# Half of gate and value by seven half products, a fixed order of instructions, and first loads in halves

## The chip, the cores and the metric

The kernel runs on one core of a Trainium2 chip. The metric is the device time of one execution in microseconds; lower is better. Three timed runs of the kernel before gave 265.98, 265.60 and 265.23 us, a median of 265.6 us. A core has a matrix engine (TensorE, PE in the profile), two engines for elementwise work (VectorE, DVE; ScalarE, ACT), a general engine (POOL) and one that mostly issues transfers (SP). Each takes its own instructions in order; they wait for one another by semaphores. Matmuls write into PSUM, eight banks of 512 float32 per partition, and both elementwise engines read from there.

## The reference

```python
# causal attention: q, k, v are [4 batches, 8 heads, 768 tokens, 64]
scores = matmul(q, k.transpose(0, 1, 3, 2)) / 8
# heads 0, 2, 6: every key up to the query
# the other five: the last 64 keys and the first 4 ("sinks")
a = softmax(where(mask, scores, -1e9))
x = matmul(a, v)                       # -> [3072 tokens, 512]
# feed-forward, weights 512 x 1536, 512 x 1536, 1536 x 512, 512 x 512
g   = x @ w_gate
val = x @ w_val
ffn = (gelu(g) * val) @ w_out
out = x + sigmoid(x @ w_res) * ffn
```

## The kernel before

**Tiling.** The 3072 tokens are six chunks of 512 (CHUNKS), numbered 0 to 5. A chunk's attention is computed for pairs of heads, then its feed-forward, while the attention of the next chunk is mixed in between. Everything that TensorE multiplies is float16, sums are float32.

**Stages of a chunk.** Queries and keys are brought into transposed form, by TensorE for the first chunks (`loads_rows`, L672; qks staging tiles, qkt results) and by transposing transfers of SP for the later ones (`loads_natural`, L732, dT). Scores go to PSUM (L893, sink scores L984), ACT takes the exponential (L909), VectorE masks. TensorE weighs the values (L1017 for the windows of streaming heads). The windows of 64 keys need the values shifted by 64 rows, which a copy `vs` makes from the value tile `va` (by ACT or VectorE for the first chunk, by SP's transfers later, L662). The keys and queries of head pair 1 are wanted on the lower partitions too; the transfer `q6` (L762) moves them. VectorE normalises; x stays in `xtok` as float32, and TensorE transposes a float16 copy to `xT` (L1106), 4 blocks of 128 features by 512 tokens.

**Gate and value.** `gate_value` (L1121) handles the 1536 features in twelve blocks of 128 (f = 0 to 11). For each block gate and value are 4 matmuls of 128x128 by 512 tokens each (one for each of 4 blocks of x's features), through the helper `mm` (L514 to L517). In the later chunks `mm` splits a matmul into two of 64 columns, so as to keep the tile shape of the attention's matmuls next to it; that is L517, the full one is L516. ACT takes gelu from the gate's bank to `gact` (L1166), VectorE multiplies it with the value's bank and 0.5 into `hT` (L1168).

**Output.** Two token tiles of chunk 0 use the plain product (`output`). All others use `output_fast` (L1212): for two tiles of 128 tokens, [h] · w_out is cut into halves three ways (tokens, the inner 1536 features in even and odd blocks, 256 columns) and made of seven half products instead of eight (the form of Strassen and Winograd). With A the tokens' halves and B the weights', it needs sums of h (`sums`, L1175: S1 to S4, four VectorE instructions per part, L1187), sums of w_out (`weight_sums`, L1199: T1 to T4 in `wt`, four planes), copies of partial results from PSUM to an output tile `otile` (keep, L1251 and L1252) and additions to it (plus, L1257). Then come x @ w_res with tanh (srs, L1226), the gated product (L1281), the addition of x (L1286) and a transfer of 256 KB to `out` (L1292) by SP: 128 tokens x 512 columns each.

**Loads.** POOL issues all loads from HBM (`dma`, L577): these cast float32 to float16. SP issues what moves inside the core and the outputs. The first loads are, in POOL's order: queries and keys of chunk 0 for heads 0 to 3, then for heads 4 to 7 (4 loads of 512 KB), its four value tiles, the first third of w_gate and of w_val, and so on; w_res and w_out follow.

**What sets the order.** The program is a list of tasks with dependencies. `schedule` (L219) plays them through with modelled durations and picks for each free engine the ready task with the lowest priority value; for TensorE a task that keeps the tile shape goes first. `HINTS` (L49) overwrites some priorities by task number. Tasks made with `flex` (copies out of PSUM, some additions) go to the engine that would be done sooner. Buffers come out of pools (SBUF tiles, PSUM banks by kind) at the moment when a task is scheduled. A loop at the end adds orders between a chunk's phases (gate-value after scores, the next chunk's scores after block 10). `warm` matmuls (L1333) fill the time until the first gate product.

Of the kernel before, what the change touches and what calls it, by code (L numbers as in the profile page):

```python
# [4 lines left out]
NHEAD = 8  # L5
SEQ = 768
# [37 lines left out]


HINTS = (
    "3:-58.9 11:-130.04 428:854.14 430:718.61 444:2782.08 457:-821.9 460:407.45 490:4205.68 521:1522.06 "
    "591:-818.43 610:-36.63 612:486.89 613:-2965.25 619:1544.03 621:-44.07 643:467.87 644:-881 646:4.3 656:119.6 "
    "664:25.04 673:629.62 675:-109.25 695:-2674.26 696:-1856.67 703:-881.5 706:-108.75 707:714.39 708:1939.7 "  # L49
    "711:270.02 712:497.18 716:476.22 720:652.56 738:638.32 743:520.23 744:3053.24 749:514.3 750:1799.28 "  # L50
    "751:2383.53 756:521.28 762:1469.72 764:4344.87 767:2237.74 787:-603.93 815:5053.25 817:2978.67 821:1231.87 "
    "824:1484.86 836:2402.62 837:798.1 841:706.04 848:-288.52 849:2997.07 876:2751.74 906:2555.54 913:1516.93 "
    "918:2437.99 919:1519.88 924:1537.25 931:1510.23 936:2384.32 949:2443.79 955:2089.28 967:2846.74 995:-227.38 "
    "1001:29.83 1002:3171.86 1003:3180.29 1004:1146.58 1007:2686.58 1012:1781.89 1040:-803.29 1043:1907.45 "
    "1045:1028.83 1046:667.33 1050:3229.28 1051:1536.45 1053:3573.03 1056:-1823.77 1084:4090.27 1110:2454.97 "
    "1111:2597.62 1117:2808.38 1123:2507.5 1128:2481.58 1129:2529.63 1134:2508.5 1146:2434.73 1152:2779.33 "
    "1153:3034.61 1158:3861.94 1165:2795.06 1171:3076.63 1176:2997.8 1185:5989.69 1188:2243.92 1189:2528.84 "
    "1192:2789.39 1193:2537.45 1194:3836.22 1208:3021.15 1215:6294.68 1263:3219.13 1268:5037.38 1283:4420.5 "
    "1308:4756.92 1311:3513.6 1317:3517.03 1321:3052.3 1329:5930.49 1330:3507.5 1335:3508.5 1336:3519.22 "
    "1341:4624.14 1345:3444.6 1353:3516.64 1354:3538.83 1357:2761.66 1365:3787.63 1366:5173.04 1372:5102.72 "  # L60
    "1386:5438.32 1392:4014.31 1393:4933.66 1418:5146.68 1430:4133.91 1441:5428.8 1452:5127.54 1457:2188.42 "
    "1462:4595.33 1464:5711.23 1467:9389.54 1468:4425.54 ~1471:550.69 1476:5611.77 1499:4504.13 1513:6742.83 "
    "1516:5340.27 1522:4510.5 1523:4585.63 1526:3632.38 1534:4503.02 1539:4253.34 1550:4463.64 1565:7711.51 "
    "1570:4506.5 1571:5085.34 1580:2427.42 1594:2466.44 1610:9272.71 1625:3048.93 1627:6036.71 1629:6167.81 "
    "1631:5064.12 1644:6476.5 1662:4125.72 1671:5044.95 1672:7314.6 1676:4967.2 1683:6427.71 1692:9540.12 "
    "1711:7387.16 1757:5137.62 1784:5507.1 1797:5469.41 1803:7562.23 1817:7773.49 1818:7478.69 1823:7672.83 "
    "1834:7419.08 1836:10250.4 1849:7490.55 "
)

# [31 lines left out]
class Buf:  # L101
    __slots__ = ("pool", "kind", "slot", "left", "users", "war", "free_at")

    def __init__(self, pool, kind=None):
        self.pool, self.kind = pool, kind
        self.slot = None
        self.left = 0
        self.users = []
        self.war = []
        self.free_at = 0.0  # L110


class Pool:
# [14 lines left out]

    def take(self, buf, t):
        best = min(x for x in self.free if x[0] <= t)  # L130
# [13 lines left out]
class Psum:  # L144
# [23 lines left out]

    def take(self, buf, t):
# [18 lines left out]
SWITCH = 0.1  # L188
SWAP = -3000.0
VK_AT = -18.5  # L190
VS_DMA = 0
LAT = {"pe": 0.20, "act": 0.10, "dve": 0.08, "pool": 0.12, "sp": 0.1}


# [1250 lines left out]
```

The softmax here doesn't subtract the row's maximum and nothing guards it: scores larger than these inputs give would overflow.

## Time and profile before

| | |
|---|---|
| timed runs | 265.98, 265.60, 265.23 us |
| profiled execution: span from first to last instruction | 263.7 us |
| around the span (median of the runs less the span) | 1.9 us |
| TensorE busy | 257.7 us, 3226 matmuls |
| VectorE, ACT, POOL busy | 181.6, 147.2, 89.3 us |
| gelu on ACT (L1166), 512 wide | 68 x 597 ns |
| product on VectorE (L1168), 512 wide | 68 x 686 ns |
| transfers | 29.22 MB, 111 GB/s in the mean |

The profile comes from one execution, whose own time beside its span isn't listed; the 1.9 us are a difference between it and other executions. A busy share is a mean over the span; which engine sets the end is read from the chain of work that ended last. An engine's busy time is made of instructions that may overlap: TensorE's matmuls are pipelined, so the distance between two starts is the price of one, and not its length. Times of groups are given as a sum and a mean of one; the shapes behind a group tell which rows may be compared.

### The profile page before, as it was taken

What the parts mean: (1) busy time and instruction counts of PE and PEld (TensorE: products, weight loads), DVE (VectorE), ACT (ScalarE), POOL (GpSimd) and SP (SyncE); (2) the same over time, 40 slices, a digit from 0 to 9 for tenths busy, and PEclk for the clock granted to TensorE, in tenths of its full rate; (3) what the DMA queues carried; (4) which work ended last, traced back from release to release, by engine and by line L of the source; (5) the groups of instructions that cost most, each with busy time, mean ns of one, the idle gap of its engine ahead of it and who ended that gap; (6) DMA issues with size and microseconds to landing.
All of it is one profiled execution on the core that took longest, in us unless ns stands there. A gap on an engine that the chain in (4) does not pass through costs nothing.

```text
span 263.7 us, 7495 instructions
## 1 busy us (share of the span) xinstructions
PE 257.7 (98%) x3226; PEld 164.0 (62%) x3226; DVE 181.6 (69%) x378; ACT 147.2 (56%) x237; POOL 89.3 (34%) x127
## 2 busy tenths in 40 slices
PE   7999999999999999999999999999999999999993
PEld 6777655468444668544567444589655588655692
DVE  2698437798447888557898366888557689837655
ACT  2785467974244987423787242967243888233430
POOL 8999979506109973975000000000000000000003
PEclk9999999999999999999999999999999999999999
DMA  6999999999999999999996110004200004200003
GB/s 83 174 204 206 188 175 231 175 153 204 134 200 148 165 137 177 171 179 176 174 156 150 42 40 0 2 26 101 82 2 0 2 2 122 82 2 0 2 35 127
DMA packets 96513, 29.22 MB, mean 111 GB/s; under 512 B 84449, under 2 KB 93025, under 8 KB 96481
## 3 DMA queue, kind: packets, MB, share of 16 engines
q0 software_dynamic: 70320, 14.69, 67.5%
q1 hardware_dynamic: 26160, 14.07, 28.0%
q8 instruction: 25, 0.41, 0.7%
q14 instruction: 8, 0.06, 0.1%
HBM read 29.36 MB, written 6.29 MB: 135 GB/s over the span
## 4 chain that ended last, share of the span: by engine, by line
PE 95%; DMA 2%; DVE 1%; issue 0%; POOLq 0%
PE ps L516 50%; PE ps L517 32%; PE ps L893 5%; PE ps L1333 2%; PE ps L1017 2%; PE ps L709 2%; DMA qks<-in_q_dram 2%; PE ps L1106 2%; PE ps L984 1%; DVE otile L1281 1%; DVE otile L1286 1%; DVE otile L1257 0%; POOLq L1427 0%
## 5 line engine op out<-in xcount | busy, mean ns | idle before, releaser
L1166 ACT ACTIVATE gact<-ps 128x512 f16<-128x512 f32 x68 | 40.2, 597 | 73.5 <-PE ps L516 43.7
L1168 DVE SCALAR_TENSOR_TENSOR hT<-gact,ps 128x512 f16<-128x512 f16 x68 | 46.1, 686 | 48.0 <-PE ps L516 23.1
L516 PE MATMUL ps<-xT,wg 128*128 128x512 f16 (+1 forms) x208 | 50.0, 363 | 0.0
L516 PE MATMUL ps<-xT,wv 128*128 128x512 f16 (+1 forms) x202 | 49.0, 362 | 0.0
L1286 POOL TENSOR_TENSOR otile<-otile,xtok 128x256 f32<-128x256 f32 x3 | 2.4, 801 | 136.2 <-DVE otile L1281 136.2
L577 POOL DMA_DIRECT2D qks<-in_k_dram x36 | 28.0, 810 | 17.3 <-DMA qkt<-qks 13.9
L516 PEld LDWEIGHTS ps<-xT,wg 128*128 128x128 f16 x208 | 20.1, 98 | 20.0 <-DVE otile L1257 0.3
L516 PEld LDWEIGHTS ps<-xT,wv 128*128 128x128 f16 x202 | 19.4, 98 | 20.0 <-DVE hT L1168 0.5
L577 POOL DMA_DIRECT2D qks<-in_q_dram x36 | 28.4, 828 | 2.2 <-issue 1.4
L517 PE MATMUL ps<-xT,wv 128*64 128x512 f16 x204 | 28.3, 380 | 0.0
L577 POOL DMA_DIRECT2D va<-in_v_dram x24 | 21.3, 920 | 15.1 <-PE ps L516 15.1
L517 PE MATMUL ps<-xT,wg 128*64 128x512 f16 x192 | 26.3, 379 | 0.0
L909 ACT ACTIVATE ea<-ps 128x1024 f16<-128x1024 f32 (+2 forms) x24 | 21.1, 915 | 1.7 <-PE ps L893 1.6
L1257 DVE TENSOR_TENSOR otile<-otile,ps 128x256 f32<-128x256 f32 x33 | 13.6, 417 | 7.1 <-PE ps L517 4.7
L1226 ACT ACTIVATE srs<-ps 128x512 f32<-128x512 f32 x22 | 13.1, 595 | 9.1 <-PE ps L517 6.7
L517 PEld LDWEIGHTS ps<-xT,wv 128*64 128x64 f16 x204 | 11.5, 110 | 9.8 <-DVE hT L1168 0.3
L1084 DVE TENSOR_TENSOR xtok<-ps,rcp 128x512 f32<-128x512 f32 (+1 forms) x28 | 16.8, 606 | 0.2
L517 PEld LDWEIGHTS ps<-xT,wg 128*64 128x64 f16 x192 | 11.1, 110 | 9.0
L893 PE MATMUL ps<-qkt 64*128 64x64 f16 (+4 forms) x391 | 16.4, 213 | 0.0
L893 PEld LDWEIGHTS ps<-qkt 64*128 64x128 f16 x391 | 9.8, 94 | 8.0 <-issue 4.2
L516 PE MATMUL ps<-wo,hT 128*128 128x256 f16 (+1 forms) x84 | 14.4, 304 | 0.0
L1286 DVE TENSOR_TENSOR otile<-otile,xtok 128x512 f32<-128x512 f32 (+1 forms) x21 | 14.3, 691 | 0.2
(109 smaller groups left out, 437.4 us busy)
## 6 DMA issues: line engine op xcount, KB each, us to landing
out_dram<-otile SPq DMA_DIRECT2D x22, 256.0 KB, 2.4
va<-in_v_dram POOLq DMA_DIRECT2D x24, 128.0 KB, 17.6
qks<-in_k_dram POOLq DMA_DIRECT2D x32, 64.0 KB, 12.6
qks<-in_q_dram POOLq DMA_DIRECT2D x32, 64.0 KB, 13.0
wg<-in_moe_w_gate_dram POOLq DMA_DIRECT2D x3, 512.0 KB, 10.2
wv<-in_moe_w_val_dram POOLq DMA_DIRECT2D x3, 512.0 KB, 12.1
wo<-in_moe_w_out_dram POOLq DMA_DIRECT2D x4, 384.0 KB, 22.8
vs<-va SPq DMA_DIRECT2D x4, 260.0 KB, 7.9
```

The lines of the kernel that those rows point to most:

```text
L516: return e.matmul(o, lhsT=lhsT, rhs=rhs, **k)
L517: return [e.matmul(o[h:h + 64], lhsT=lhsT[:, h:h + 64], rhs=rhs, **k) for h in (0, 64)][-1]
L577: return G.add(eng, issue, lambda e: e.dma_start(out_ap(), in_ap), deps, prio, bufs=bufs, dma=cost, name=name, grp=grp)
L709: return [e.transpose(out=at16(scr)[64 * x:64 * x + 64, (m * n + i) * 128:(m * n + i + 1) * 128], in_=piece(jj, h, i), identity=ident[:, : ...
L893: return [e.matmul(at(scr)[:, oo:oo + w], lhsT=side(BB, low, 1)[half, k0:k0 + 128], rhs=side(BB, low, 0)[half, qq:qq + w], start=True, sto ...
L909: return e.activation(out=o, in_=i_, func=AF.Exp, scale=SM_SCALE)
L1084: t2 = G.add("dve", c_dve(2 * n * 64), lambda e: e.tensor_tensor(out=xview(), in0=avv(0, DHEAD), in1=scale(), op=ALU.mult), [t1] + xdeps, ...
L1166: ta = G.add("act", c_act(512), (lambda gb=gb, ga=ga: lambda e: e.activation(out=at(ga)[:, :], in_=at(gb)[:, :], func=AF.Gelu))(), [tg], p ...
L1168: th = G.add("dve", c_dve(512), (lambda vb=vb, ga=ga, f=f: lambda e: e.scalar_tensor_tensor(out=hv(f), in0=at(ga)[:, :], scalar=0.5, in1=a ...
L1226: tas.append(G.add("act", c_act(512), (lambda rb=rb, sr=sr: lambda e: e.activation(out=at(sr)[:, :], in_=at(rb)[:, :], func=AF.Tanh, scale ...
L1257: return G.add("dve", c_dve(256), lambda e: e.tensor_tensor(out=dst(), in0=dst(), in1=at(D)[:, 0:256], op=ALU.add), [t, k], pr, bufs=[D, o ...
L1286: fn = (lambda ot=ot, lt=lt, w=w: lambda e: e.tensor_tensor(out=at(ot)[:, w], in0=at(ot)[:, w], in1=at(xbuf)[:, lt, w], op=ALU.add))()
```

## The change

1. **Seven half products for the blocks 6 to 11 of gate and value, chunks 1 to 5** (`fast`). Blocks 6, 7, 8 are paired with 9, 10, 11. For each pair, gate and value each become one group: halves of the tokens (256), of x's features (two blocks of 128) and of the output features (the two blocks). Each product is two matmuls of 128x128 by 256. Three *lanes* of two PSUM banks hold the groups in turn. Between the products a copy within PSUM (seed), a copy to an `otile` buffer (hold) and two additions (merge) do what keep and plus do in `output_fast`. The sums of x (xS, four per chunk) and of the weights (`gv_sums`, eight in all, T3 in place of the weight block) are made by VectorE. gelu and product then read both halves of a block from the two banks of the lane in one instruction.
2. **Fixed order.** `HINTS` is empty. `PLAN` lists for each engine the numbers of its tasks in order (TensorE, ACT, VectorE, POOL, SP) and for each buffer its place. `schedule` follows the lists. The loop over phases is gone; some modelled durations differ.
3. **First chunk's queries and keys** are loaded in halves of 256 tokens: six loads in POOL's order, the second half of the queries (512 KB) ahead, then keys and queries of the first half for heads 0 to 3 and 4 to 7 (256 KB each), then the keys' second half. qkt is split into a tile for keys and one of 512 wide for a chunk's queries; `q6` becomes two transfers; `vs` copies seven of eight heads.
4. **x stored early in chunks 1 to 4** (ACCUM, `store_x`). SP writes x (1 MB) to `out` as soon as it is there; the 16 output tiles of these chunks then are added to it by accumulating transfers that POOL issues, and the addition of x on VectorE falls away.
5. **Small things.** w_out's T3 replaces its block, `wt` has three planes; hS is split into two tiles, the smaller shared with xS; two srs buffers instead of three; warm matmuls are 256 wide and 70 instead of 124; the last outputs may be issued by ACT's queue (one is).

In the built programs TensorE has 3434 matmuls instead of 3226, VectorE 454 instructions instead of 378, ACT 282 instead of 225, POOL 141 instead of 123, SP 72 instead of 80.

```diff
+VS = (NHEAD - 1) * (DHEAD + 1)
+NP = 3
+FA, FB = NF - 2 * NP, NF - NP
+LANES = 3
...
+PLAN = (
...
+ACCUM = range(1, 5)
...
+        lists = [[int(x) for x in line.split()] for line in "".join(PLAN).split("/")] if PLAN else []
+        queue = {e: [self.tasks[x] for x in xs] for e, xs in zip(ENGS, lists)}
+        if queue:
+            bufs = dict.fromkeys(b for t in self.tasks for b in t.bufs)
+            assert len(bufs) == len(lists[5])
+            for b, x in zip(bufs, lists[5]):
+                b.fixed = x if x >= 0 else None
...
-                for t in cand[e]:
+                offers = cand[e]
+                if queue:
+                    offers = [t for t in queue[e][heads[e]:heads[e] + 1] if t in offers] + [t for t in offers if t.name == "warm"][:1]
...
+        "lane": (LANES, [(4, 5), (2, 3), (0, 1)]),
...
+        for y in range((z - a) // 2):
+            lo = (a + 2 * y) * 128
+            for gi, (h0, h1) in enumerate(((0, 4), (4, 8)) if c == 0 and y == 0 else ((0, 8),)):
+                for j, src in ((1, k), (0, q)):
+                    t = dma("pool", base + 4 * gi + 8 * y + 1 - j, (h1 - h0) * n * (0.092 if c else 0.089),
+                            (lambda j=j, h0=h0, h1=h1, y=y: lambda: sv(j, h0, h1, y))(),
+                            src[b, h0:h1, lo:lo + 256, :].rearrange("h (p j) d -> p h (j d)", j=n), bufs=[st[j]])
+                    t.late = 1.0 if c else 0.0
+                    for h in range(h0, h1):
+                        tok[j, h, y] = t
         values(b, a, z, base + (10 if c == 0 else 2), False, c == 0)
...
+    def gv_sums():
+        for nm, w in (("g", wg), ("v", wv)):
+            wt_ = gvt[nm]
+            blk = lambda k, j: w[:, 2 * k:2 * k + 2, (FB if j else FA) * 128:(FB if j else FA) * 128 + NP * 128]
+            here = [wtok[nm, j] for j in range(3)]
+            def add(o, x, y, deps, k):
+                return G.add("dve", c_dve(NP * 256, 2, False), lambda e: e.tensor_tensor(out=o, in0=x, in1=y, op=ALU.subtract),
+                             deps, 910 + k, name=f"{nm}T")
+            t1 = add(wt_[:, 0], blk(0, 1), blk(0, 0), here, 0)
+            t2 = add(wt_[:, 1], blk(1, 1), wt_[:, 0], [t1] + here, 1)
+            t4 = add(wt_[:, 2], blk(1, 0), wt_[:, 1], [t2] + here, 2)
+            t3 = add(blk(0, 1), blk(1, 1), blk(0, 1), [t1] + here + gv_tail, 3)
+            gvtok[nm] = {"T1": t1, "T2": t2, "T3": t3, "T4": t4}
...
+        for q in range(2 * NP):
+            j, nm = q // 2, "gv"[q % 2]
+            fa, fb, w, wt_ = FA + j, FB + j, (wg, wv)[q % 2], gvt[nm]
+            blk = lambda k2, f, w=w: lambda k: w[:, 2 * k2 + k, f * 128:(f + 1) * 128]
+            tw = lambda x, wt_=wt_, j=j: lambda k: wt_[:, x, k, j * 128:(j + 1) * 128]
+            right = {"B11": blk(0, fa), "B21": blk(1, fa), "B22": blk(1, fb), "T3": blk(0, fb), "T1": tw(0), "T2": tw(1), "T4": tw(2)}
+            lane = lanes_[q % LANES]
+            ps, free = lane
+            es = Buf(P_ot)
+            AL, AR, BL, BR = (slice(x * 256, x * 256 + 256) for x in range(4))
+            name, p_ = f"{nm}{fa}", pr + 6 + q
+            def product(parts, deps, extra=(), ps=ps, left=left, right=right, name=name, p_=p_):
+                need = [x for l, r, _, _ in parts for x in ([stok[l]] if l[0] == "S" else xd) + ([gvtok[nm][r]] if r[0] == "T" else [])]
+                t = G.add("pe", c_mm(256, 2 * len(parts)), lambda e: [
+                    mm(e, at(ps)[:, D], lhsT=right[r](k), rhs=left[l](k), start=first and k == 0, stop=(k == 1), skip_group_check=True)
+                    for l, r, D, first in parts for k in range(2)], need + deps, p_, bufs=[ps, xtbuf, xs] + list(extra), name=name)
...
+            def copy(o, i, deps, bufs, nm_):
+                return G.flex({"act": (c_act(256), lambda e: e.activation(out=o(), in_=i(), func=AF.Copy)),
+                               "dve": (c_dve(256), lambda e: e.tensor_copy(out=o(), in_=i()))}, deps, p_, bufs=bufs, name=nm_)
+            def merge(o, deps, ps=ps, es=es):
+                return G.add("dve", c_dve(256), lambda e: e.tensor_tensor(out=at(ps)[:, o], in0=at(ps)[:, BL], in1=at(es)[:, 0:256], op=ALU.add),
+                             deps, p_, bufs=[ps, es], name="merge")
+            t15 = product([("A11", "B11", AL, True), ("S1", "T1", AR, False)], list(free))
+            seed = copy((lambda ps=ps: at(ps)[:, BL]), (lambda ps=ps: at(ps)[:, AL]), [t15], [ps], "seed")
+            hold = copy((lambda es=es: at(es)[:, 0:256]), (lambda ps=ps: at(ps)[:, AR]), [seed], [ps, es], "hold")
+            t6 = product([("S2", "T2", BL, False)], [seed])
+            m1 = merge(AR, [t6, hold])
+            t7 = product([("S3", "T3", BL, False)], [m1])
+            t23 = product([("A12", "B21", AL, False), ("S4", "B22", AR, False)], [m1])
+            m2 = merge(BR, [t7])
+            t4 = product([("A22", "T4", BL, False)], [m2])
...
+                if nm == "g":
+                    ga = gas[f] = Buf(P_ga)
+                    ta = G.add("act", c_act(512), (lambda x=x, ga=ga, both=both: lambda e: e.activation(
+                        out=two(at(ga)[:, :]), in_=both(x), func=AF.Gelu))(), done + [t4], p_, bufs=[ps, ga], fset="gelu", name=f"gelu{f}")
...
+        t1 = add(wt[:, 0], w(0, 1), w(0, 0), tall, 1)
+        t2 = add(wt[:, 1], w(1, 1), wt[:, 0], [t1], 2)
+        add(w(0, 1), w(1, 1), w(0, 1), tall + [t1] + plain, 3)
+        add(wt[:, 2], w(1, 0), wt[:, 1], [t2], 4)
...
+    def store_x(c, xbuf, xtoks):
+        n = 2 if c == len(CHUNKS) - 1 else 4
+        r0 = c * 512
+        stored[c] = G.add("sp", 0.65, lambda e: e.dma_start(
+            out[r0:r0 + n * 128, :].rearrange("(i p) d -> p i d", p=128), at(xbuf)[:, 0:n, :]),
+            list(dict.fromkeys(t for i in range(n) for t in xtoks[i])), 1000 * c - 3500, bufs=[xbuf], dma=0.65 * n, name="xst")
+        stored[c].late = 1.0
...
+            if c in ACCUM and not end:
+                t = G.add("pool", 1.0, (lambda ot=ot, r0=r0: lambda e: e.dma_start(out[r0:r0 + 128, :], at(ot)[:, :], accum_op=ALU.add))(),
+                          ends + [stored[c]], pr - 3000, bufs=[ot], dma=1.0, name="out")
+                t.late = 2.0 if c < 4 else 1.5
+                continue
...
+        if c in ACCUM:
+            store_x(c, xbuf, xtoks)
```

## The prediction

> **What bounds the kernel now.** I read the page first, then the chain in order of time, TensorE's timeline, single stretches, and last the groups with their shapes.
>
> ```profile
> span 263.7 us, 7495 instructions
> ...
> PE 257.7 (98%) x3226; PEld 164.0 (62%) x3226; DVE 181.6 (69%) x378; ACT 147.2 (56%) x237; POOL 89.3 (34%) x127
> ...
> PEclk9999999999999999999999999999999999999999
> DMA  6999999999999999999996110004200004200003
> ...
> PE 95%; DMA 2%; DVE 1%; issue 0%; POOLq 0%
> ```
>
> TensorE is busy 98% and makes 95% of the chain, at full granted clock in every slice. The transfers are near their limit for the first 22 slices (145 us) and idle after. The chain in order of time (start, length, what) says where TensorE is not the bound:
>
> ```profile
> 1.32 4.32 DMA qks<-in_q_dram
> ...
> 24.92 11.25 PE ps L516 x64
> ...
> 105.16 0.03 issue
> ...
> 257.37 0.42 DVE otile L1257
> ...
> 259.33 1.01 DVE otile L1281 x3
> 260.37 0.77 DVE otile L1286
> ```
>
> Up to 24.9 us it waits for loads; from there to 259.3 us no link names another engine for more than a few hundredths; then follows a tail of 4.3 us. So between 24.9 and 259.3 us a microsecond of matmul removed is a microsecond won, unless a new wait eats it. Two prices come from TensorE's timeline (start, length, what):
>
> ```profile
> 68.69 1.03 PE L516 MATMUL ps<-xT,wg 128*128 128x512 f16 x4
> 69.55 1.03 PE L516 MATMUL ps<-xT,wv 128*128 128x512 f16 x4
> ...
> 93.67 0.82 PE L516 MATMUL ps<-wt,hT 128*128 128x256 f16 x6
> 94.42 0.61 PE L893 MATMUL ps<-qkt 64*128 64x128 f16 x10
> ```
>
> Starts count, not lengths. Four matmuls of 512 columns take 69.55 − 68.69 = 0.86 us, 216 ns each. Six of 256 take 0.75 us: 6 × 109 ns (their spacing inside the group) plus about 0.10 us, which every change of the tile's shape (here 128*128 to 64*128) costs. Pairs of 64-column matmuls (the late chunks) cost per pair the same as one full matmul. With these prices for every matmul in the written order I get 245.1 us for TensorE's stream; the trace is that stream shifted by 12.3 us at the dense start and 14.2 us at the end, so under 2 us of waits lie between.
>
> **The change part by part, against the profiled execution's 263.7 us of span.**
>
> *Seven half products.* One group covers gate (or value) of two 128-feature blocks for 512 tokens. Before: 2 × 4 matmuls of 512 = 8 × 216 = 1.728 us. After: 7 products × 2 = 14 of 256 = 14 × 109 = 1.526 us. Saved 0.202 us; three pairs, gate and value, five chunks make 30 groups: −6.06 us. The new order has 106 changes of tile shape instead of 99: +7 × 0.10 = +0.7. Together **−5.4**; the new list priced in full gives 239.9 us, −5.2.
>
> Here a rule speaks against the change. "TensorE: Matmul & The Clock Gate" of the Trainium skill, section "Back-to-back issue gap", gives for a sustained stream of weight load and matmul about 81 ns at 128 columns and 131 ns at 512, that is some 98 ns at 256 between them. By it a group goes from 8 × 131 = 1.05 to 14 × 98 = 1.37 us, 30 × 0.32 = +9.7 us, and the kernel to about 275. The rows decide: 216 and 109 ns are measured in this stream, weight loads included, so a half-width matmul costs half.
>
> *What each group asks of the others.* A copy from PSUM to PSUM (seed), one to an output tile (hold), and two additions (merge) on VectorE. Nearest rows by shape:
>
> ```profile
> L1257 DVE TENSOR_TENSOR otile<-otile,ps 128x256 f32<-128x256 f32 x33 | 13.6, 417 | 7.1 <-PE ps L517 4.7 <-PE ps L516 2.0
> L1286 DVE TENSOR_TENSOR otile<-otile,xtok 128x512 f32<-128x512 f32 x20 | 13.4, 684 | 0.2
> ...
> L1187 DVE TENSOR_TENSOR hS<-hT 128x512 f16<-128x512 f16 x6 | 2.6, 426 | 0.2
> ```
>
> A 256-wide ACT copy out of PSUM takes 0.380 us (L1252). VectorE: 60 merges × 0.417 = 25.0, 16 seeds and holds × 0.42 = 6.8, 20 sums of x × 0.42 = 8.4, eight weight sums × 0.55 (between the 0.42 of 512 and the 0.95 of 1536 elements, L1204) = 4.4; away go 16 additions of x × 0.684 = 10.9, about eight keeps that move to ACT (3.4), and some 2.9 of smaller copies: 181.6 + 27.4 = 209 us. ACT: 44 seeds and holds × 0.38 = 16.7, the keeps 3, small things 1.9: 147.2 + 21.6 = 169 us. In the stretch of chunk 3 (stretch and length; busy PE, weight loads, VectorE, ACT, POOL; granted clock, DMA share, GB/s):
>
> ```profile
> 128.14:165.25 37.11, 37.11 (x356) 21.63 (x357) 27.00 (x55) 20.91 (x32) 0.00 (x0) 1.00 0.57 88
> ```
>
> VectorE goes from 27.0 to 27.0 + 12 × 0.417 + 4 × 0.42 + 3 × 0.42 − 4 × 0.684 = 32.2 us, in a chunk that shrinks to about 36: 90%. It fits, with little room.
>
> *New waits.* TensorE takes its list in order. Product 6 waits for the seed, 7 and the 2+3 pair for the first merge, 4 for the second: 90 waits, and whatever stands behind on TensorE waits too. One link costs 0.20 us (last matmul to the engine's start, as before a gelu) + 0.38 to 0.42 + 0.05 back = 0.64 to 0.68 us. In the new order other matmuls stand between the steps: at least 0.87 us nearly everywhere, 0.65 once. That is the cover; without it 90 × 0.65 = +58 us. About 30 of the waits have 0.9 us or less, where one instruction of 0.69 us just begun on VectorE makes it late. Ends: 0, and 30 × 0.12 = +3.6 (half of 0.69 less the 0.23 of margin). The nearest row is the output stage, which already lives with copies and additions between its products, and where TensorE shows no idle time with VectorE at 73% of the chunk; so near the lower end: **+0.4**.
>
> *First loads in halves.* The order on POOL's queue becomes: six loads of queries and keys, two value tiles, w_val's first third, a query load of chunk 1, two value tiles, w_gate's first third. Before, the first two weight loads landed at 16.88 and 19.43 us, and the first gate product started at 19.72, behind 7.37 us of other matmuls. Now w_gate has 512 KB more ahead of it (1.43 us by the first loads' landing intervals): about 21 to 22 us; the first gate product has 1.9 us more matmuls ahead of it and would start at 21.6 with before's gaps. Ends −0.3 and +0.9; I take **+0.3**. That the first scores can start earlier only moves work within this wait.
>
> *Shifted values of chunk 1.* Their copy waits for value tiles which now stand behind w_out's four loads. Counting POOL's bytes at the 175 GB/s of those slices, the tiles land near 52 us; a copy on SP's queue takes 5.3 to 8 us (page: 7.9 median), so 57.3 to 59; the windows of chunk 1 want it at 57.8. Before it landed at 45.1 for a need at 56.4. Ends 0 and +2.5; **+0.6**.
>
> *x stored early, outputs accumulated.* Four stores of 1 MB on SP, which stand ahead of transposes, vs and q6 of the next chunk there; and 16 accumulating outputs on POOL, ahead of one value and two query loads of chunk 3. "DMA: Bandwidth & Descriptors" of the skill, section "Issuing engines are not separate DMA queues", says that all issuers share the same engines and interleave; the trace agrees where both queues are at work (the 9s of the DMA row). So the store of chunk 1 costs the loads about 6 us (1 MB at 175 GB/s) rather than nothing. Chunk 2's q6 had 1.24 us of slack (landed 88.56, used 89.79); now I put need at 90.5 and landing at 85 to 90: ends 0 and +3, **+0.2**. Chunk 3 had over 15 us, and after slice 22 the engines idle. The queries behind the accumulating outputs keep an estimated 7 us.
>
> *The rest at nothing.* The first chunk's weight sums run beside its output matmuls; two result buffers instead of three and the split hS stand under the same matmuls; the tail stays at 4.3 us, since the last four outputs keep their additions; fewer warm-ups only fill the wait for loads.
>
> Sum: −5.4 + 0.4 + 0.3 + 0.6 + 0.2 = −3.9. Span 263.7 − 3.9 = 259.8; the timed runs lie 1.9 us above the span (median 265.6), so **261.7 us**.
>
> **The rivals.**
> *All waits covered.* Only the stream's −5.4 counts: 260.2. For it: no idle on TensorE before. Against it: three tight places at once.
> *VectorE becomes the bound in the gate-value stage.* 30 late merges × 0.12 = +3.6 instead of 0.4: 264.9, anywhere from 263.2 to 266. For it: 90% load and 30 thin covers; against it: ACT can carry seeds, and the stage between (scores, windows) lets VectorE catch up.
> *Slower: POOL's queue stops at the first accumulating output.* It waits for the store of x and for chunk 1's last gated value; behind it stand chunk 3's queries. If the store lands late (it shares the engines with all loads), the scores of chunk 3 start late. From about 7 us late it costs time, from 11 us late it has eaten the 3.9; at 14 us late the kernel takes about 268.7. For it: 9s in the DMA row until 145 us; against it: those loads need only be in at about 127 us.
> *The folding does not do what it says* (half-width matmuls at more than half the price, as in the rule above): 275, and the 109 ns row excludes it.
>
> **How the numbers follow.** The likeliest case (260.6 to 263.2) 0.54; all covered 0.20; VectorE the bound 0.15, of which 0.05 end within 0.8 us of before; POOL's queue 0.10; anything else 0.01. 0.3% of 265.6 is 0.8 us, about what a measurement of this kernel tells from no change. Faster: 0.54 + 0.20 + 0.10 and the odd 0.01 = 0.85; same 0.05; slower 0.10. The range goes from below the covered case (all ends low: −5.4 − 0.3, 259.9, and 0.3 of spread) to 264.6, where most of the third case is in.
>
> **What would show it.** Right: matmul starts 109 ns apart in the new groups; TensorE's busy time near 252 us at 97 to 98%; VectorE near 209, ACT near 169; TensorE idle before the products with merges and seeds under 0.5 us in sum, before the first gate product at 21 to 22 us, before chunk 1's windows near 57 us. Wrong: idle before the merged products in every chunk with VectorE at 95% (third case), idle before the scores of chunk 3 released by a DMA (fourth), or a later dense start than 26 us.

## The result

The changed kernel is slower: over the runs of one chip its ratio to the kernel before is 1.0056 (95% interval 1.0033 to 1.0079), medians 268.54 and 265.84 us. The ratio leaves out its three longest executions (270.48, 272.1 and 275.8 us), which count as slow because they lie over 1.5% above its fastest; the medians are of all seven. Its executions scatter much more (266.2 to 275.8 us, before 265.2 to 266.8), and the profiled one, at 270.48 us, is among the longer; the reading below says which waits vary. In a later comparison the same kernel had 1.0201 (1.0141 to 1.0262).

The page of the profile after:

```profile
span 268.7 us, 8098 instructions
...
PE 255.6 (95%) x3434; PEld 180.5 (67%) x3434; DVE 206.6 (77%) x454; ACT 165.6 (62%) x293; POOL 106.6 (40%) x145
...
PEclk9999999999999999999999799999999999999999
DMA  7999999998989999999909999347473019340004
...
PE 70%; DMA 14%; POOL 11%; ACT 2%; issue 2%; DVE 1%; POOLq 0%; DVEq 0%
```

TensorE is no longer 95% of the chain but 70%; transfers and POOL, which issues them, hold a quarter. The transfer row has 9s up to 168 us (slices of 6.7 us; before up to 138 us), with an empty slice from 134 to 141 us, and the slice after 148 us shows a lower TensorE clock. What TensorE waited for in the whole execution, its three largest waits (engine, line, releaser: us in total, times, longest):

```profile
PE ps L616 <- DMA xT<-x: 2.2, 1, 2.2
PE ps L1137 <- issue: 2.0, 1, 2.0
PE ps L1137 <- DMA vs<-va: 1.3, 1, 1.3
...
```

Three single waits, none on a merge. The chain in order of time places them:

```profile
31.15 21.46 DMA va<-in_v_dram
...
52.62 7.84 DMA vs<-va
...
60.51 0.44 PE ps L1137 x16
...
141.83 8.45 DMA xT<-x
150.32 9.89 PE ps L616 x50
...
226.09 1.96 issue
228.04 0.35 PE ps L1137 x11
```

At 60.5 us chunk 1's windows wait for the shifted values; at 150.3 us chunk 3's gate products wait for transposed x, a transfer that took 8.45 us (3.2 us in the median before); at 226 us TensorE stops for 2 us in the middle of a group, waiting for nothing that the profile shows.

TensorE's stream, priced as in the prediction, is 239.9 us, and the trace follows it except at a few places. The *shift* is how much later a matmul starts in the trace than it would if the stream ran without a wait. The first row gives the streams, the second the shift at the dense start, each later row what is added to the time in that stretch (us; the last matmul's 0.1 us stands in the first row and in the last but one):

| stretch | before | after | difference |
|---|---|---|---|
| stream of matmuls | 245.1 | 239.9 | −5.2 |
| shift at the dense start (27 us) | 12.42 | 13.99 | +1.6 |
| 27 to 62 us (chunk 1's windows) | 0.26 | 1.50 | +1.2 |
| 62 to 140 us | 0.72 | 1.11 | +0.4 |
| 140 to 151 us (chunk 3's transposed x) | 0.04 | 2.43 | +2.4 |
| 151 to 162 us (lower clock, one merge) | 0.0 | 1.93 | +1.9 |
| 162 us to the last matmul, without the next | 0.81 | 0.70 | −0.1 |
| the stop at 226 us | 0.0 | 2.2 | +2.2 |
| from the last matmul's start to the end | 4.4 | 5.1 | +0.7 |
| span | 263.7 | 268.7 | +5.0 |

This is the account of one long execution. Without the two rows from 140 to 162 us its span would be 264.4 us and its time 266.2 us (1.8 us lie around this span: 270.48 − 268.7); the fastest execution took 266.15 us. So by this estimate the start, chunk 1's windows, the stop at 226 us and the tail already cancel the gain, and the two rows are most of the scatter. No short execution of this kernel was profiled, so this is a fit and not a measurement.

The lower clock, in TensorE's timeline after the wait at 150 us:

```profile
150.77 2.94 PE L616 MATMUL ps<-xT,wg 128*128 128x512 f16 x8
153.50 1.70 PE L616 MATMUL ps<-xT,wv 128*128 128x512 f16 x4
155.04 0.38 PE L616 MATMUL ps<-xT,wg 128*128 128x256 f16 x2
```

Eight matmuls take 2.73 us and four 1.54, where 216 ns each would make 1.73 and 0.86; so the difference is that of eight matmuls at 0.43 us. The granted clock from 151.5 to 154.8 us is 0.50. 426.7 ns at 512 columns is what the Trainium skill ("TensorE: Matmul & The Clock Gate", section "Wait — 56ns, not 53.3ns?") gives for the cold clock, so row and page agree; the price is 1.00 + 0.68 = 1.7 us on top of the wait.

### The profile page after: what moved, and what is told of

It is laid out like the page before. It is cut to its first block, busy times and chain, and to the rows that moved or that the text cites. A ratio compares the mean times of both kernels' runs of the same rounds, so it can differ in the third digit from the quotient of the medians.

```text
span 268.7 us, 8098 instructions
## 1 busy us (share of the span) xinstructions
PE 255.6 (95%) x3434; PEld 180.5 (67%) x3434; DVE 206.6 (77%) x454; ACT 165.6 (62%) x293; POOL 106.6 (40%) x145
## 4 chain that ended last, share of the span: by engine, by line
PE 70%; DMA 14%; POOL 11%; ACT 2%; issue 2%; DVE 1%; POOLq 0%; DVEq 0%
PE ps L617 32%; PE ps L616 31%; DMA va<-in_v_dram 8%; POOL qks L678 4%; PE ps L1013 3%; DMA xT<-x 3%; DMA vs<-va 3%; POOL va L678 2%; PE ps L1137 1%; POOL wo L678 1%; PE ps L1226 1%; POOL wg L678 1%; POOL wv L678 1%; POOL m_win L636 0%; ACT L1111 0%
## 5 line engine op out<-in xcount | busy, mean ns | idle before, releaser
L1523 POOL DMA_DIRECT2D out_dram<-otile x16 | 14.9, 1014 | 87.8 <-DVE otile L1519 77.6
L616 PE MATMUL ps<-xT,wg 128*128 128x512 f16 (+1 forms) x172 | 40.1, 344 | 0.0
L616 PE MATMUL ps<-xT,wv 128*128 128x512 f16 (+1 forms) x162 | 37.2, 341 | 2.2 <-DMA xT<-x 2.2
L678 POOL DMA_DIRECT2D qks<-in_k_dram x37 | 31.4, 873 | 10.4 <-DMA kT<-qks 10.4
L1366 DVE TENSOR_TENSOR ps<-ps,otile 128x256 f32<-128x256 f32 x60 | 24.7, 429 | 7.2 <-PE ps L616 3.4
L616 PEld LDWEIGHTS ps<-xT,wv 128*128 128x128 f16 x162 | 15.8, 99 | 14.4 <-DMA xT<-x 2.7
L1029 ACT ACTIVATE ea<-ps 128x1024 f16<-128x1024 f32 (+2 forms) x24 | 21.4, 920 | 3.2 <-PE ps L1013 3.2
L617 PE MATMUL ps<-xT,wv 128*64 128x512 f16 (+1 forms) x164 | 20.1, 346 | 0.0
L616 PE MATMUL ps<-wo,hT 128*128 128x256 f16 (+1 forms) x114 | 19.2, 296 | 0.2 <-ACT otile L1490 0.2
L617 PE MATMUL ps<-xT,wg 128*64 128x512 f16 (+1 forms) x144 | 17.7, 344 | 0.0
L1013 PE MATMUL ps<-qT,kT 64*128 64x64 f16 (+4 forms) x391 | 16.6, 213 | 0.0
L1362 ACT ACTIVATE ps<-ps 128x256 f32<-128x256 f32 x26 | 9.6, 370 | 9.5 <-PE ps L616 6.3
```

The lines of the kernel that those rows point to most:

```text
L616: return e.matmul(o, lhsT=lhsT, rhs=rhs, **k)
L617: return [e.matmul(o[h:h + 64], lhsT=lhsT[:, h:h + 64], rhs=rhs, **k) for h in (0, 64)][-1]
L678: return G.add(eng, issue, lambda e: e.dma_start(out_ap(), in_ap), deps, prio, bufs=bufs, dma=cost, name=name, grp=grp)
L1013: return [e.matmul(at(scr)[:, oo:oo + w], lhsT=side(BB, qb, low, 1)[half, k0:k0 + 128], rhs=side(BB, qb, low, 0)[half, qq:qq + w], start=T ...
L1029: return e.activation(out=o, in_=i_, func=AF.Exp, scale=SM_SCALE)
L1366: return G.add("dve", c_dve(256), lambda e: e.tensor_tensor(out=at(ps)[:, o], in0=at(ps)[:, BL], in1=at(es)[:, 0:256], op=ALU.add), deps, ...
```

## The experiments

Orders are changed by a list MOVE of (engine, task, task ahead of which it goes); all else stays. Each run's ratio is to the kernel before, run beside it.

**a1_again: the changed kernel once more.**

> The changed kernel once more, unchanged, for a profile of an ordinary execution. Theory (late transfers): TensorE's stream of 239.9 us is followed without stalls except at transfers: about 1 to 1.4 us before the windows of chunk 1, 0 to 2.3 us before the gate products of chunk 3 (their transposed x), and the time varies by several us from execution to execution because that wait varies. Rival (VectorE is the bound in the gate-value stage): the waits stand before products with merges, in every chunk, some 3 us in sum, the same in each execution.

271.52 us, 1.0201 (1.0141 to 1.0262), from four executions, on the chip that also ran b1_plain_out, c1_values and d1_queue. Why the same kernel came out at 1.0056 before stays open; gains against a1_again would be 3.9 us smaller against that ratio (0.0145 x 266). The waits: 1.6 us before chunk 1's windows, 0.7 us for chunk 3's transposed x, 2.2 us at 228 us, and one of 1.7 us at 161 us that is put down to a merge. After the first and the third the granted clock was 0.50 (62.5 to 65.8 and 229.7 to 233.0 us), which cost about 1.6 us each time. VectorE's timeline at 161 us:

```profile
157.91 0.42 DVE L1366 TENSOR_TENSOR ps<-ps,otile 128x256 f32<-128x256 f32 x1
160.28 0.43 DVE L1363 COPY otile<-ps 128x256 f32<-128x256 f32 x1 [1.95 <-DMA out_dram<-otile]
160.81 0.77 DVE L1366 TENSOR_TENSOR ps<-ps,otile 128x256 f32<-128x256 f32 x2
```

The hold stood for 1.95 us because its otile buffer was still being read by an accumulating output, which took 10.4 us to land (issued 149.88, landed 160.25). So this is a late transfer too, and not VectorE as the bound. The waits that end with a semaphore stand at transfers and change from run to run, as the first theory says; the stop at 228 us has none.

**b1_plain_out: part 4 undone alone.** A triple of ADDS is an output's number, the VectorE task ahead of which its addition goes, and the SP task ahead of which its transfer goes. The two xtok tiles then have to alternate.

```diff
-ACCUM = range(1, 5)
+ACCUM = ()
+ADDS = ((873, 939, 333), (876, 939, 333), (902, 986, 334), (905, 1033, 315), (1114, 1158, 1183), (1117, 1149, 1183), (1146, 1243, 338), (1143, 1224, 341), (1349, 1428, 406), (1346, 1487, 387), (1375, 1454, 387), (1582, 1584, 1657), (1585, 1672, 1859), (1378, 1565, 1657), (1614, 1716, 1859), (1611, 1691, 1859))
...
+            for c, b in enumerate(self.xbufs):
+                b.fixed = c % 2
```

> Part 4 undone alone: no early store of x, the 16 outputs as plain transfers from SP's queue, the 16 additions on VectorE, a chunk's x kept until then. Late transfers: POOL's queue no longer stands at 129 to 140 us, 4 MB fewer are moved, the wait of chunk 3's gate products goes (2.3 us and up to 1.7 us of lower clock after it), 262 to 264 us. Rival (VectorE): 10.9 us more on VectorE (206.6 to 217), more late merges, 269 us or more.

266.40 us, 1.0018 (0.9998 to 1.0038): 5.1 us faster than a1_again beside it, although VectorE has 9 us more (215.8). After the start only one of TensorE's waits is left in size, that of chunk 1's windows; the transposed x is in time and nothing stops at 226 us:

```profile
PE ps L1147 <- DMA vs<-va: 1.4, 1, 1.4
```

So on this chip the stores and accumulating outputs cost more than the additions that they save; against the first comparison's 1.0056 the gain is 1.0 us. It came out 2.4 us above the theory's range: the start (14.9 us of shift) stayed late, and waits of 0.2 to 0.5 us behind VectorE and ACT are new.

**d1_queue: POOL's order alone, chunk 2's outputs behind eleven loads.** In the changed kernel POOL's timeline has a hole of 10 us ahead of the accumulating output:

```profile
128.40 1.07 POOL L1523 DMA_DIRECT2D out_dram<-otile  x1
139.61 0.87 POOL L1523 DMA_DIRECT2D out_dram<-otile  x1 [10.14 <-DVE ea L1065]
140.26 2.07 POOL L678 DMA_DIRECT2D va<-in_v_dram  x2
```

The output waited for its data from VectorE. The loads behind it did not have to wait (in d1_queue they are issued from 129.5 us on without one), and here they run when chunk 3's transpose of x does.

```diff
+MOVE = (('pool', 382, 1114), ('pool', 385, 1114), ('pool', 358, 1114), ('pool', 391, 1114), ('pool', 389, 1114), ('pool', 361, 1114),
+        ('pool', 377, 1114), ('pool', 372, 1114), ('pool', 357, 1114), ('pool', 376, 1114), ('pool', 388, 1114))
...
+        for e, x, y in MOVE:
+            queue[e].remove(self.tasks[x])
+            queue[e].insert(queue[e].index(self.tasks[y]), self.tasks[x])
```

> POOL's order alone: eleven loads that stood behind the accumulating outputs of chunk 2 (from 129.5 us on POOL waited 10 us for the first of them) are issued ahead of these outputs. If the queue's order is the cause of the wait before chunk 3's gate products, these loads land by about 145 us and the wait falls from 2.3 us to under 0.7, without the lower clock after it: 2 to 4 us faster than the changed kernel in a disturbed execution. If the bytes of the x stores and outputs are the cause, the wait stays.

267.19 us, 1.0043 (1.0018 to 1.0068), 4.3 us faster than a1_again. The eleven loads now fill the hole and have landed by 143.6 us (in the changed kernel between 146.7 and 167.7 us), and TensorE's waits at 150 and 161 us are gone; the stop near 222 us is left:

```profile
PE ps L1143 <- issue: 2.7, 1, 2.7
```

The profiled execution, at 269.37 us, is the longest of nine: the granted clock was 0.50 at 11.1 to 14.4 us and again at 226.2 to 229.4 us, after that stop.

**d2_bytes: the bytes alone.** The early stores write 32 of 512 columns, so the output lacks the rest of x.

```diff
-            out[r0:r0 + n * 128, :].rearrange("(i p) d -> p i d", p=128), at(xbuf)[:, 0:n, :]),
+            out[r0:r0 + n * 128, 0:32].rearrange("(i p) d -> p i d", p=128), at(xbuf)[:, 0:n, 0:32]),
```

> The changed kernel with its own order, but each early store of x writes only 32 of the 512 columns (the output lacks the rest of x): 3.9 MB fewer on the transfer engines. If the bytes make the waits of chunk 3 (transposed x, and the copies that need an output tile back), they go: 266 us or less. If it is POOL's order (ten us of standing at 129 us), they stay as in a1_again: 270 us.

267.77 us, 1.0072 (1.005 to 1.0093): between the two expectations, and not settled by time, since a1_again did not run beside it and the changed kernel's own ratio was 1.0056 once and 1.0201 once. In the trace the wait for transposed x is 0.7 us (2.2 and 0.7 us with all bytes), there is none in size for an output tile (1.7 us in a1_again alone), and the stop at 222 us is 1.3 us. The first two lie within what the two profiles with all bytes show, so whether the bytes take part is not shown. That POOL's order does is: with it mended, in d1_queue and the kernels built on it, the wait for x was nothing in d1_queue, e1_fetch, f2_start and g1_all, and 1.0 to 1.2 us in f1_values and h1_gates.

In all profiles this wait follows the time of the transposing transfer itself, from issue to landing. At 3.2 to 6.3 us there is no wait; 7.0 us (a1_again, d2_bytes) goes with 0.7, 7.3 (f1_values) with 1.0, 7.5 (h1_gates) with 1.2, 8.3 (c1_values) with 2.1 and 8.45 us (the changed kernel) with 2.2.

**c1_values: chunk 0's last value tiles and chunk 1's earlier.**

```diff
+MOVE = (('pool', 218, 200), ('pool', 219, 200), ('pool', 292, 404), ('pool', 296, 404), ('pool', 286, 404), ('pool', 289, 404))
```

> POOL's order alone: the first chunk's third and fourth value tile ahead of the first third of w_val; chunk 1's value tiles ahead of four query and key loads that are wanted 20 us later. Late transfers: the dense start comes 1 us earlier (13.98 us after the stream's own time becomes about 13), the wait of 1.3 us before chunk 1's windows goes; 2 us faster than the changed kernel. Rival (the first wait is set by w_gate's landing at 21.4 us, which this doesn't move): only the 1.3 us.

271.50 us, 1.0235 (1.019 to 1.0281), no better than a1_again. The wait before chunk 1's windows did go. But the start came later (shift 15.6 us): POOL also builds the window mask between its loads, and with two loads ahead of it the last instruction of the mask ran at 13.98 us instead of 12.2. And chunk 3 waited 2.1 us for x and 3.5 us for an output tile. An order that helps in one place is paid elsewhere on the same queue.

**e1_fetch: d1_queue with one accumulating output earlier.** The stop near 225 us came at the same matmul, the 2880th, in every profile with two or three outputs in flight. In c1_values and f2_start, where more warm matmuls ran, the 2880th was another instruction of the program, and the stop came there. That is how a boundary in the instruction stream looks. The trace also has the packets of the queue that brings instructions, 16 KB each (it does not tell for which engine), and the one nearest to the stop starts as follows:

```
kernel        outputs just issued   fetch starts   last matmul before   2880th matmul
after                 3                225.76           225.89            228.04
a1_again              3                226.61           226.47            228.87
d1_queue              3                222.96           222.42            225.26
c1_values             3                227.82           228.51            230.52
d2_bytes              3                221.42           222.41            223.90
e1_fetch              2                220.15           221.93            222.89
f1_values             2                221.53           222.46            223.98
f2_start              2                223.17           223.29            225.74
g1_all                1                218.21           220.66            220.76
h1_gates              1                219.42           221.83            222.26
b1_plain_out   0 (plain, by SP)        221.78           224.33            224.34
```

TensorE goes on 2.3 to 2.8 us after the packet's start where it had to wait; in g1_all and b1_plain_out, where the packet started about 2.5 us ahead of the last matmul, it didn't wait. The number of outputs alone does not set the stop: f2_start had 2.3 us with two, d2_bytes 1.3 with three.

```diff
...
+        ('pool', 1378, 1582))
```

> As d1_queue, and the third of the accumulating outputs that were issued together at 220 us goes ahead of the other two (its data is ready at 210 us). In all runs with accumulating outputs TensorE stood still for 2.0 to 2.8 us at 225 to 230 us in the middle of a group of matmuls, at the same count of matmuls, waiting for no semaphore. Theory (its next instructions are fetched by a transfer that queues behind these outputs): with fewer of them in flight the stall falls below 1 us, 265 to 266 us. Rival (the fetch is slow at this place by itself): it stays at 2 to 3 us, 267 us.

265.54 us, 0.9963 (0.9945 to 0.9981): faster than before, for the first time. The stop is 0.8 us:

```profile
PE ps L1143 <- issue: 0.8, 1, 0.8
```

That the packet is TensorE's, and that it queues behind the outputs, is inferred from the table, from this change and from g1_all; the queueing itself isn't seen, only when the packet starts.

**e4_unfold: part 1 undone, on b1_plain_out.**

```diff
-            t15 = product([("A11", "B11", AL, True), ("S1", "T1", AR, False)], list(free))
...
+            t15 = plain(fa, (0, 1), L, list(free))
+            t6 = plain(fa, (2,), L, [], [es])
+            t7 = plain(fa, (3,), L, [])
+            t23 = plain(fb, a, R, [])
+            t4 = m2 = plain(fb, b, R, [])
```

> As b1_plain_out, and part 1 undone in the same order list: blocks 6 to 11 by plain matmuls of 512 columns, without sums of x and weights, copies and merges. Theory (the fold saves what the two prices say, and its waits are hidden): 30 x 0.202 = 6.1 us slower than b1_plain_out, less some 1 us of small waits that go: 271 to 272.5 us. Rival (waits for copies and merges eat the gain): within 2 us of b1_plain_out.

271.77 us, 1.0213 (1.0194 to 1.0233), against b1_plain_out's 1.0018: the fold is worth 0.0195 x 266 = 5.2 us. TensorE's stream differs by 5.9 us; the fold's waits in b1_plain_out cost the 0.7 between. VectorE falls from 215.8 to 176.5 us and the time does not fall with it, so all but those 0.7 us of its load is hidden:

```profile
PE 261.2 (97%) x3180; PEld 162.7 (60%) x3180; DVE 176.5 (65%) x366; ACT 150.3 (56%) x249; POOL 92.1 (34%) x129
```

**e2_first and e3_best: the first loads whole again.** On b1_plain_out, four loads of 512 KB in rows of 1 KB, transposed pair by pair (the order of these transposes was written anew); e3_best has chunk 1's values of c1_values too.

```diff
-            for gi, (h0, h1) in enumerate(((0, 4), (4, 8)) if c == 0 and y == 0 else ((0, 8),)):
...
+FIRST = (('pool', (211, 210, 213, 212)), ('pe', (230, 228, 408, 234, 232, 411, 238, 236, 242, 240, 422)), ...)
+        n = 4 if c == 0 else 2
```

> As b1_plain_out, and the first chunk's queries and keys come as before the change: four loads of 512 KB with rows of 1 KB, transposed pair by pair. Theory (part 3 delays the start: the last of these loads landed at 11.1 to 12.3 us instead of 9.7): it lands at 9.7 again, the dense stream starts at 12.5 to 13 us after its own time instead of 14.9, 264 to 264.5 us. Rival (the start is set by the value tiles and w_gate that land at 20 and 22 us): no change, 266.4 us.

> As e2_first, and four query and key loads of POOL's queue go behind chunk 1's value tiles. Late transfers: the wait of 1.4 us before chunk 1's windows goes too: 262.5 to 263.5 us, faster than both kernels. Rival (an earlier start only makes the loads later against it): the wait stays or grows, 264 us or more.

267.88 and 267.90 us, 1.0066 and 1.0065. The last of these loads landed at 10.1 us in e2_first instead of 11.5 in b1_plain_out, and yet the dense stream started later (shift 17.4 instead of 14.9). So that theory falls: within this plan, going back to whole loads does not bring the start forward. What the loads and what the new order of transposes add to these 2.5 us isn't told apart. Chunk 1's windows no longer waited in either, because they came later; e3_best therefore tells nothing on the values.

**f1_values: e1_fetch with chunk 1's values earlier.**

```diff
...
+        ('pool', 292, 404), ('pool', 296, 404), ('pool', 286, 404), ('pool', 289, 404))
```

> As e1_fetch, and four query and key loads that are wanted 20 us later go behind chunk 1's value tiles on POOL. Late transfers: the wait of 1.2 to 1.6 us before chunk 1's windows goes, 264.2 us. Rival: the start of the dense stream decides and the wait only moves, 265.5 us.

264.71 us, 0.9958 (0.9935 to 0.9981), by ratio no better than e1_fetch. The windows' wait is gone, but in the profiled execution 1.0 us for chunk 3's x and 1.3 us at 222 us took it back.

**f2_start: a first try at the start**, moves ('pool', 199, 200), ('pool', 218, 200), ('pool', 219, 200), ('pool', 245, 200), ('act', 226, 513), ('act', 227, 513) on f1_values.

> As f1_values, and the start reordered: on POOL w_gate's first third and the first chunk's third and fourth value tile go ahead of w_val's first third and of chunk 1's query load; on ACT the two copies of shifted values, which wait for these tiles, go behind the four copies of transposed x. Theory (the fixed order lists delay the start: first gate product at 23.2 us with w_gate landing at 21.4 to 23.1 us and ACT held for a value tile): the dense stream starts 1 to 1.5 us earlier, 263 us. Rival (the start is bound by the chain scores, exponential, weighing itself): no change.

268.80 us, 1.0112 (1.0081 to 1.0142). The moved loads stood ahead of the mask constants again; the first weighing came at 16.0 us instead of 13. It says nothing on the theory.

**g1_all: the same with the constants in place, and one more output later.**

```diff
...
+        ('pool', 1585, 1611), ('pool', 199, 200), ('pool', 218, 245),
+        ('pool', 245, 223), ('pool', 200, 201), ('act', 226, 513), ('act', 227, 513))
```

> As f1_values (the changed kernel with POOL's order mended around chunk 1's values and chunk 2's outputs), and two things that the trace shows apart. At the start, with the mask constants kept at their places (they were late in c1_values and f2_start): w_gate's first third takes the place of w_val's, the third value tile that of chunk 1's query load, and ACT's two copies of shifted values go behind the four copies of transposed x. If POOL's and ACT's fixed order delays the dense start, it comes 1 to 1.5 us earlier (14.0 instead of 15.1 us after the stream's own time); if the chain of scores, exponential and weighing is the bound, no change. Near 222 us: one more of the outputs goes later, so that only one is in flight when TensorE's instructions are fetched: the stall there of 1.0 to 1.5 us goes. Together 262 to 263 us; 263.3 if the start doesn't move.

263.66 us, 0.9926 (0.99 to 0.9951), the fastest. After the start TensorE has one named wait left, of 0.2 us; the stop at 222 us is gone:

```profile
...
PE ps L831 <- POOL ident L642: 1.1, 1, 1.1
PE ps L831 <- DMA qks<-in_k_dram: 0.6, 1, 0.6
PE ps L622 <- ACT otile L1496: 0.2, 1, 0.2
```

But the start did not move (shift 14.7; with the old order it was 14.0 to 15.1). w_gate's third now landed at 17.0 us and the first gate groups had their inputs at 21.3 us; they stood in TensorE's list behind windows that waited for the copies of shifted values until 23.0 us.

**h1_gates: the first three gate groups ahead of those windows**, ('pe', 530, 486), ('pe', 522, 486), ('pe', 514, 486) on g1_all.

> As g1_all, and in TensorE's list the first three gate groups go ahead of the second half's windows. In g1_all these groups had their inputs at 21.3 us and stood in the list behind windows that waited for a copy of shifted values until 23.0 us. If the fixed order is what delays the dense start, it comes 1.0 us earlier (13.6 us after the stream's own time instead of 14.7): 262.6 us. If the chain of the second half is the bound, the wait moves behind the gate groups: 263.6 us.

264.37 us, 0.9942 (0.9924 to 0.9961). The first gate group came at 21.8 us instead of 24.0, but the shift at the dense start was 14.2 us, which is half of the expected gain, and the old order had given 14.0 too; a wait of 0.4 us behind it is new; in the profiled execution chunk 3's x was late by 1.2 us again. The intervals of the two overlap.

**g2_plain: b1_plain_out with the start and the values of g1_all.**

> As b1_plain_out (plain outputs from SP, no early store of x), with chunk 1's values and the start as in g1_all. Theory (late transfers): the wait of 1.4 us before chunk 1's windows goes and the start gains 1 us: 264 us. If the start doesn't move, 265 us.

265.82 us, 0.9999 (0.9982 to 1.0016), 0.8 us above the higher of the two expectations. The wait before chunk 1's windows did not go (0.9 us), and waits of 0.2 to 0.5 us, several of them behind VectorE (215.6 us), add up to about 2 us more than in g1_all. Accumulating outputs in a good order are worth 2 us over plain ones (263.66 us for g1_all beside it).

## Why the prediction was wrong

- *The fold's price (−5.4, and +0.4 for its waits): right.* The rule of 131 and 98 ns does not hold here: half-width matmuls start 109 ns apart also in the new groups, as TensorE's timeline of the changed kernel shows (two in 0.22 us):

```profile
76.51 0.38 PE L616 MATMUL ps<-wS,wgt 128*128 128x256 f16 x2
76.73 0.38 PE L616 MATMUL ps<-wS,wvt 128*128 128x256 f16 x2
76.95 0.38 PE L616 MATMUL ps<-xs,wg 128*128 128x256 f16 x2
```

  e4_unfold puts it at 5.2 us net. In the profiled execution TensorE waits only about 0.2 us at a merge (at 160.2 us). Its busy time was 255.6 us for the 252 forecast; in g1_all, without a stretch of lower clock in the stream, it was 253.6. VectorE (206.6 for 209) and ACT (165.6 for 169) came as forecast; "VectorE becomes the bound" and "the folding does not do what it says" fall.
- *First loads (+0.3): wrong, +1.6 here and +1.9 to +2.7 in the experiments' runs that kept these loads' order (+3.8 in d1_queue, with its lower clock at 11 us).* w_gate landed at 21.4 us, as estimated. The step of this term that failed is "would start at 21.6 with before's gaps": the first gate group started at 23.2, with other work that had gaps of its own (second-half scores, copies of shifted values) ahead of it in the list. How much of the loss is the list and how much the chain of chunk 0's attention stays open: one and the same order gave shifts of 14.0 to 15.1 us, so the 14.7 (g1_all) and 14.2 us (h1_gates) of the new orders show no gain, and all lie 1.6 us or more above before.
- *Chunk 1's values (+0.6): right in mechanism, low in size.* The tiles landed at 52.6 us (estimate 52), the copy took 7.8 us; it landed at 60.5 for a need at 59.1: +1.4, inside the ends given.
- *x stored early and accumulated (+0.2): the step that failed.* It was priced at chunk 2's and chunk 3's queries, and chunk 3 was set aside with "after slice 22 the engines idle". They don't. The share of the transfer engines and the rate from 140 to 151 us are the last two columns; a share is the packets' times added up over 16 engines' time, so it can pass 1. The kernel before:

```profile
140.00:151.00 11.00, 11.00 (x101) 7.19 (x98) 6.55 (x14) 5.21 (x10) 0.00 (x0) 1.00 0.33 87
```

  The changed kernel:

```profile
140.00:151.00 11.00, 8.82 (x117) 6.51 (x112) 8.14 (x19) 5.29 (x10) 10.32 (x13) 1.00 1.30 113
```

  Share 0.33 before, 1.30 after, and POOL busy for 10.3 of the 11 us where it did nothing before. A queue that had stood still pushed loads into this stretch (d1_queue); what the extra megabytes add is open. The share alone does not make the wait: it was 1.25 in e1_fetch and 1.45 in f2_start, without one. What counts is the one transfer: the rule on issuing engines, quoted in the prediction, fits with the transposed x on SP's queue taking 8.45 us for 3.35 beside POOL's loads. I applied it to loads and left out the three other users of the same engines: SP's transposes of x, output tiles that a hold wants back, and, as inferred above, TensorE's own instructions. In place of +0.2 stood 2.4 + 1.9 + 2.2 = 6.5 us in the profiled execution, the lower clock that followed included. b1_plain_out, which undoes this part alone, puts its net cost at 5.1 us against a1_again and 1.0 us against the first comparison.
- *The rival that decides the sign: right that POOL stops, wrong in where and in the victim.* POOL did stop at an accumulating output, not at the first but at one of chunk 2 (10.1 us from 129.5 us), and not for the store of x but for VectorE's data; the queries behind it were in time. (It stood 87.8 us at such outputs over the run, mostly after 155 us, when no load stood behind.) That the kernel came out slower, as this rival said, is luck in that respect. It was given 0.10.
- *The tail (0): +0.7.* The last addition starts 1.6 us after the start of the last matmul instead of 1.1, and what follows takes 3.5 us instead of 3.3.

## What to carry to other kernels

When a change moves bytes or queue entries, list every user of the transfer engines in the stretch where they land, small transposes, buffers to be returned and instruction fetches included, not only the loads; a share that falls to nothing in the profile before is only free as long as the queue ahead keeps its pace. An entry with a late dependency at the head of an in-order queue delays all that stands behind; moving eleven loads ahead of the outputs that they stood behind was worth 4.3 us against a1_again. A saving on the engine that sets the end is best checked by undoing it alone inside the new kernel: here all but 0.7 us of it was there while the whole was slower.

## What the runs showed of the hardware

- TensorE stopped for 0.2 to 2.7 us with no semaphore to wait for, always at the 2880th matmul, and went on 2.3 to 2.8 us after the start of a 16 KB instruction packet. With one or no accumulating output just issued the packet started early enough, or nearly so; that it waits behind such outputs is inferred.
- In the dense stream, waits of 1.6, 2.3, 2.4, 2.8 and 3.7 us were followed by 3.4 us at a granted clock of 0.50, which cost 1.4 to 1.7 us more; waits of 1.9, 2.15, 2.2 and 2.45 us passed without it, and waits of up to 1.4 us too. Among the warm matmuls of the start, one such stretch (d1_queue) came after a gap of 1.5 us.
- An accumulating output of 256 KB landed 3.7 to 4.2 us after its issue when alone, and up to 13.8 us (c1_values) with loads and other outputs in flight; plain ones from SP in b1_plain_out took 2.0 to 3.5 us after 140 us, and up to 5.8 us while loads were in flight.
